# A decode attention kernel on one core: K of one pair loaded in two parts, the next V load held behind the first, waits of SyncE dropped, a clear cut into 32 pieces

## The chip, the cores and the metric

The kernel runs on one core of one Trainium2 chip, while nothing else runs beside it. The time is that of the device, in microseconds (us), the median of several runs. One further execution was taken by the hardware profiler; what is said of engines, waits and transfers comes from that one.

## The reference, cut to what matters

One decode step: 8 sequences, 32 heads, 4096 cached keys of 128 elements per head, all in bf16. An attention block and a small MLP work on the same normalized input, and both are added to x.

```python
xn = layernorm(x)                                   # x: [8, 1, 640]
q = (xn @ wq).reshape(8, 1, 32, 128).transpose(0, 2, 1, 3)
scores = einsum("bhqd,bhkd->bhqk", q, k_cache) * 128 ** -0.5
o = einsum("bhqk,bhkd->bhqd", softmax(scores), v_cache)
out = x + o.transpose(...).reshape(8, 1, 4096) @ wo \
        + gelu(layernorm(xn) @ w1 + b1) @ w2 + b2
```

`k_cache` and `v_cache` are [8, 32, 4096, 128] each. Every element of both is read once, 537 MB of the 552 MB that the kernel loads.

## The kernel before

**Pairs.** The work is cut into NQ = 32 pairs, i = 0 to 31, of one sequence and 8 heads. The K of a pair is one tile of 128 partitions x 256 columns x 128 elements (8.39 MB): 16 partitions per head, 256 keys (columns) in each partition, contiguous in memory. V has the same shape. "K of pair 4" in the change is the fourth one, i = 3.

**Buffers.** `S_sb` has three slots: K goes into `KA` for even i and `KB` for odd i, V always into `VS`. So K of pair i can be loaded when K of pair i - 2 has been used, and V of pair i when V of pair i - 1 has been used.

**Loads.** All large loads are issued by SyncE (`sp`) and run in one queue spread over 16 DMA engines. `load_k(i)` waits for `kt(i-2)` (the last transpose of that K by TensorE) and `km(i-2)` (the last reduction of that K by VectorE), then issues one DMA. `load_v(i)` waits for `pv(i-1)`, the last matmul of the pair before on V, and issues one DMA (two, of 192 and 64 columns, for i = 30). wq comes ahead of all of them; the MLP's weights and wo come last.

**Scores.** Columns 0 to 175 of a K tile are multiplied and reduced on VectorE, in three chunks (`dve_chunk`, the end of each is `km`). Columns 176 to 255 are transposed by TensorE (`pe_T`), copied by ScalarE (`act_T`) and multiplied by TensorE (`pe_QK`); VectorE folds the result (`dve_sel`), and this stands in VectorE's order before the third chunk. `k_ready(i)` is a tiny memset of `kr_sb` on GpSimd that waits for K; TensorE's transposes wait for it instead of the DMA. Then follow the maximum on VectorE, the exponentials on ScalarE, `pe_PV` on TensorE (256 matmuls per pair) and the normalization on GpSimd.

**Order.** The order is written out by hand: every step has a position and each engine takes its steps in the order of positions.

```python
for i in range(NQ):
    o = i * Q                       # Q = 100
    if i:
        at(o - 51, load_k, i)
    at(o + 50, load_v, i)
    at(o - 2, k_ready, i)
```

So SyncE's queue reads wq, K0, K1, V0, K2, V1, K3, V2, K4, V3 and so on; SyncE waits for one release after the other, in this order. VectorE, ScalarE and TensorE replay their steps from loops; SyncE and GpSimd run straight-line code.

**Start.** `consts_pool` runs on GpSimd at the start: index tiles (`iota`), then `zeros_sb` (128 x 128, bf16), `ones_sb`, `mx_sb`, `mb_sb` and `ones_f`. The ticket `consts` after the last is waited for by `pe_acc0`, the first matmuls into `ACC_ps`, and by `dve_max`. The memset of `ones_sb` also raises the semaphore `ld_vl` by one, a trick by which TensorE's loop can have a wait in every turn for the second part of V of i = 30.

All instructions are recorded by helper classes, so nearly all have line 111 in the profile; they are told apart by their tiles.

Of the kernel before, what the change touches and what calls it, by code (L numbers as in the profile page):

```python
# [14 lines left out]
P = 128  # L15
# [177 lines left out]
def bass_parallel_sum__gqa_block_cached__mixer_channel_mlp__decode_kernel(  # L193
# [21 lines left out]
    NQ = NHQ * B  # L215
# [5 lines left out]
    TPB = 8  # L221
    NS = 2
    LOOP0, LOOPN = 2, 15
    assert NKEY == 256 and NQ == 32
    SLOT = NKEY * DH
    KA, KB, VS = 0, 1, 2
# [6 lines left out]
    def jp_of(i):  # L233
        return 80

    def chunks(i):
        jd = NKEY - jp_of(i)
        n = 3
        return [(jd * c // n, jd * (c + 1) // n) for c in range(n)]

    def kslot(i):
        return KA if i % 2 == 0 else KB
# [8 lines left out]
    with ExitStack() as es:  # L251
        sb = lambda name, shape, dt: es.enter_context(nc.sbuf_tensor(name, shape, dt))
        ps = lambda name, shape, dt: es.enter_context(nc.psum_tensor(name, shape, dt))
        sem = lambda name: es.enter_context(nc.semaphore(name))

        S_sb = sb("S_sb", [P, 3, SLOT], BF)
        tile = [S_sb[:, s, :].rearrange("p (j d) -> p j d", d=DH) for s in range(3)]
# [6 lines left out]
        def scratch(n, rows=P, slot=KB):  # L264
            ap = part(slot, o_[slot], n, rows)
            o_[slot] += n + n % 2
            return ap
# [22 lines left out]
        zeros_sb = scratch(P)  # L290
        assert max(o_.values()) <= SLOT

        ones_sb = sb("ones_sb", [1, B], BF)
# [17 lines left out]
        mx_sb = sb("mx_sb", [P, 32], F32)  # L311
        mxT_sb = sb("mxT_sb", [P, 32], F32)
        mq_sb = sb("mq_sb", [P, 2], F32)
        mb_sb = sb("mb_sb", [P, 32], F32)
# [23 lines left out]
        pe, dve, act, sp, pool = (_Eng(sem(f"{n}_s")) for n in ("pe", "dve", "act", "sp", "pool"))  # L338
        pe2, act2 = _Eng(sem("pe2_s")), _Eng(sem("act2_s"))
        ld_s = [_Dma(sem(f"ld_s{s}")) for s in range(3)]  # L340
        ld_x, ld_b1, ld_b2, ld_wq, ld_w1, ld_w2a, ld_w2b, st_o = (
            _Dma(sem(n)) for n in ("ld_x", "ld_b1", "ld_b2", "ld_wq", "ld_w1", "ld_w2a", "ld_w2b", "st_o"))
        ld_vl = [_Dma(sem(f"ld_vl{q}")) for q in range(1, len(V_CUT) - 1)]
        ld_wl = [_Dma(sem(f"ld_wl{q}")) for q in range(2)]
        ld_wn = [_Dma(sem(f"ld_wn{q}")) for q in range(len(WN_CUT) - 1)]
        tk = {}
# [5 lines left out]
        def load(key, dma, dst, src, eng=None):  # L352
            tk[key] = dma.sig((eng or sp).dma_start(dst, src))

        def cache_src(cache, i):
            hq, b = divmod(i, B)
            return cache[b, hq * HS:(hq + 1) * HS].rearrange("h (p j) d -> (h p) j d", j=NKEY)

        def load_k(i):
            s = kslot(i)  # L360
            if i >= 2:
                sp.wait(tk[("kt", i - 2)], tk[("km", i - 2)])
            elif s == KB:
                sp.wait(tk["qmm"])
            tk[("k", i)] = ld_s[s].sig(sp.dma_start(tile[s], cache_src(A_k_cache, i)))

        def load_mlp():
            sp.wait(tk[("kt", NQ - 2)], tk[("km", NQ - 2)])
            load("w1", ld_w1, w1_sb, B_w1.rearrange("(p c) f -> p c f", c=DC))
            load("w2a", ld_w2a, w2_sb, B_w2[0:FB * P, :].rearrange("(p c) n -> p c n", c=FB))  # L370

        def load_v(i):
            sp.wait(tk["qmm"] if i == 0 else tk[("pv", i - 1)])
            if i != NQ - 2:
                tk[("v", i)] = [ld_s[VS].sig(sp.dma_start(tile[VS], cache_src(A_v_cache, i)))]
                return
            tk[("v", i)] = []
            for d, lo, hi in zip([ld_s[VS]] + ld_vl, V_CUT[:-1], V_CUT[1:]):
                if lo:
                    d.n += 1  # L380
                tk[("v", i)].append(
                    d.sig(sp.dma_start(tile[VS][:, lo:hi, :], cache_src(A_v_cache, i)[:, lo:hi, :])))
# [3 lines left out]
            load("b1", ld_b1, b1_sb, B_b1.rearrange("(o f) -> o f", o=1), act)  # L386

        def load_wl(q):
            sp.wait(tk[("kt", NQ - 1)], tk[("km", NQ - 1)])
            lo, hi = (0, HW) if q == 0 else (HW, HW + HS)  # L390
            tk[("wl", q)] = ld_wl[q].sig(sp.dma_start(
                woW_sb if q == 0 else woL_sb[:, 0, :],
                A_wo[lo * DH:hi * DH, :].rearrange("(p s) n -> p (s n)", p=P)))
# [15 lines left out]
        def consts_pool():  # L409
            pool.iota(iota_h, [[-HP, HS]], base=0, channel_multiplier=1)  # L410
            pool.iota(iota_w, [[-RW, HW]], base=0, channel_multiplier=1)
            tk["iota"] = pool.sig(pool.iota(iota_i, [[1, P]], base=0, channel_multiplier=-1))
            for d, (ap, v) in zip([None] + ld_vl + [None] * 2, (
                    (zeros_sb, 0.0), (ones_sb[:, :], 1.0), (mx_sb[:, :], 0.0), (mb_sb[:, :], 0.0))):
                inst = pool.memset(ap, v)
                if d is not None:
                    inst.call[3] = (d.sem, 1)
            tk["consts"] = pool.sig(pool.memset(ones_f[:, :], 1.0))
# [124 lines left out]
                qT_sb[:, hq * HS:(hq + 1) * HS, b][:, :, None].to_broadcast([P, HS, HP])))  # L543

        def k_ready(i):
            pool.wait(tk[("k", i)])
            tk[("kr", i)] = pool.sig(pool.memset(kr_sb[:, :], 0.0))

        def pe_qbc(i):
# [242 lines left out]
        at(-898, load, "b2", ld_b2, b2_sb, B_b2.rearrange("(o f) -> o f", o=1), act)  # L792
        at(-890, load, "wq", ld_wq, wq_sb, A_wq.rearrange("(p c) n -> p c n", c=DC))
        at(NQ * Q - 55, load_mlp)
        at(-897, load_w2b)
        at(-870, load_k, 0)
        at(-899, zero_w2b)
        at(-800, consts_pool)
        at(-795, idents)
        at(NQ * Q - 60, sel_pool)  # L800
# [15 lines left out]
        for i in range(NQ):  # L816
            o = i * Q
            last = i == NQ - 1
# [3 lines that stand above are left out]
            at(o - 52, qrep, i)  # L822
            at(o - 2, k_ready, i)
            at(o - 11, pe_qbc, i)
            at(o - 10.5, act_qbc, i)
            nt = jp_of(i) // TPB
            w = 42.0 / nt
            for t in range(nt):
                at(o + w * t, pe_T, i, t)
                at(o + w * (t + 0.4), act_T, i, t)  # L830
                at(o + w * (t + 1.5), pe_QK, i, t)
            at(o + 2, dve_chunk, i, 0)
            at(o + 26, dve_chunk, i, 1)
            at(o + 52, dve_sel, i, 0)
            at(o + 55, dve_sel, i, 1)
            at(o + 58, dve_chunk, i, 2)
            at(o + 84, dve_max, i)
            at(o + 90 if i else o + Q + 45, act_exp, i)
            at(o + Q + 48, pe_RS, i)
            at(o + Q + 57, dve_rinv, i)  # L840
            at(o + Q + 50, pe_PV, i)
            if not last:
                at(o + Q + 71, act_O, i)
            at(o + Q + 75, o_norm, i)
# [4 lines left out]
        for q in range(2):  # L849
            at(o + 50 + 0.1 * q, load_wl, q)  # L850
            at(o + 79.1 + 0.2 * q, fin_wl, q)
# [73 lines left out]
```

## Time and profile before

| | |
|---|---|
| median of 3 runs | 1282.03 us (1281.86 to 1282.14) |
| the profiled execution, from its first to its last instruction (its own time) | 1280.5 us |
| the median less that span | 1.5 us |
| busy: VectorE, TensorE matmul, ScalarE, GpSimd | 1103.8 (86%), 671.1 (52%), 476.6 (37%), 106.3 us (8%) |
| loaded from memory | 551.80 MB, 431 GB/s over the span |
| share of the 16 DMA engines taken by SyncE's queue | 99.7% |

In the lines of the profile, PE is TensorE's matmul, DVE VectorE, ACT ScalarE, POOL GpSimd, and SP SyncE; a q behind a name (SPq) is the engine's sequencer, which issues DMAs. A line of a timeline gives the start, the duration, the engine and operation, what is written from what, and in brackets the idle time ahead of it with what ended it. A line of the list of waits gives the total, the count and the longest. Times are in us from the span's start. DMA packets are counted where they start.

### The profile page before, as it was taken

Reading aid. Unit: us, or ns where it says so; the run is one execution under the profiler, and the core shown is the slowest. Engines: PE = TensorE matmul, PEld = TensorE weight load, DVE = VectorE, ACT = ScalarE, POOL = GpSimd, SP = SyncE. Lnnn points to the kernel's source line nnn. Section 1 sums busy time; section 2 is a strip of 40 time slices with the busy share of each in tenths; the row PEclk is TensorE's granted clock in tenths of the full one; section 3 lists DMA queues with packets and bytes.
Section 4 is the critical chain, followed back from the end, with each engine's and each line's share of the span. In section 5 each row is a group of like instructions: output and inputs, shape, how many; then the busy total and the mean of one; then the engine's idle time right before and its main releaser. Section 6 shows DMA issues by size and latency. Waiting matters only on the chain.

```text
span 1280.5 us, 34440 instructions
## 1 busy us (share of the span) xinstructions
PE 671.1 (52%) x13944; PEld 573.4 (45%) x13944; DVE 1103.8 (86%) x680; ACT 476.6 (37%) x904; POOL 106.3 (8%) x113
## 2 busy tenths in 40 slices
PE   1546555446545446545456554456454466464476
PEld 1435444335535345444345444345343355353365
DVE  1899999889888889888899888898888898888895
ACT  0524444233444233443234443234443234442331
POOL 0020010000000000000000000000000000000040
PEclk9755655566665565555565565566655555555655
DMA  9999999999999999999999999999999999999998
GB/s 419 431 426 435 426 436 432 442 426 436 432 440 428 434 432 438 432 432 430 436 438 426 434 434 442 426 434 434 438 430 430 430 440 436 428 432 436 433 437 361
DMA packets 10675, 551.99 MB, mean 431 GB/s; under 512 B 1244, under 2 KB 1445, under 8 KB 1702
## 3 DMA queue, kind: packets, MB, share of 16 engines
q1 hardware_dynamic: 10512, 551.70, 99.7%
q8 instruction: 9, 0.15, 0.0%
q10 hardware_dynamic: 150, 0.11, 0.0%
q14 instruction: 4, 0.03, 0.0%
HBM read 551.80 MB, written 0.01 MB: 431 GB/s over the span
## 4 chain that ended last, share of the span: by engine, by line
DMA 52%; DVE 36%; issue 11%; DVEq 0%; PE 0%; SPq 0%; ACT 0%
DMA S_sb<-in_A_k_cache_dram 51%; DVE S_sb L111 26%; DVE Sd_sb L111 8%; DMA S_sb<-in_A_wo_dram 2%; DVE S_ps L111 1%; DVE ri_sb L111 0%; DVEq L109 0%; PE ACC_ps L111 0%; DVE mx_sb L111 0%; SPq L111 0%; DVE mbT_sb L111 0%; DVE mxT_sb L111 0%; DVE mq_sb L111 0%; DVE mb_sb L111 0%; PE QB_ps L111 0%
## 5 line engine op out<-in xcount | busy, mean ns | idle before, releaser
L111 PE MATMUL TR_ps<-ident_bf,S_sb 128*128 128x128 bf16 (+1 forms) x2570 | 341.2, 273 | 354.1 <-POOL kr_sb L111 333.7
L111 DVE TENSOR_TENSOR S_sb<-S_sb,qbc_sb 128x7552 bf16<-128x7552 bf16 (+1 forms) x96 | 392.5, 4088 | 128.8 <-DMA S_sb<-in_A_k_cache_dram 128.4
L111 PEld LDWEIGHTS TR_ps<-ident_bf,S_sb 128*128 (+2 forms) x2570 | 243.6, 102 | 414.0 <-issue 338.2
L111 DVE TENSOR_REDUCE Sd_sb<-S_sb 128x59 f32<-128x3776 bf16 (+1 forms) x96 | 390.2, 4065 | 6.0
L111 ACT ACTIVATE KT_sb<-TR_ps 128x1024 bf16<-128x1024 bf16 x320 | 327.0, 1024 | 121.1 <-PE TR_ps L111 109.5
L111 PE MATMUL PV_ps<-P_sb,S_sb 128*128 128x8 bf16 x8192 | 224.0, 175 | 137.5 <-DMA S_sb<-in_A_v_cache_dram 134.5
L111 PEld LDWEIGHTS PV_ps<-P_sb,S_sb 128*128 128x128 bf16 x8192 | 221.4, 103 | 140.2 <-DMA S_sb<-in_A_v_cache_dram 137.0
L111 DVE TENSOR_TENSOR S_sb<-S_sb 128x3776 bf16<-128x3776 bf16 (+1 forms) x96 | 205.4, 2140 | 3.3
L111 ACT ACTIVATE P_sb<-Sd_sb,NB_sb 128x256 bf16<-128x256 f32 x256 | 126.3, 494 | 213.7 <-DVE NB_sb L111 213.7
L111 PE MATMUL S_ps<-qrep_sb,KT_sb 128*128 128x8 bf16 x2560 | 121.6, 177 | 51.6 <-ACT KT_sb L111 48.6
L111 ACT ACTIVATE oU_sb<-PV_ps 128x8 f32<-128x8 f32 x31 | 5.5, 178 | 376.8 <-PE PV_ps L111 376.8
L111 PEld LDWEIGHTS S_ps<-qrep_sb,KT_sb 128*128 128x128 bf16 x2560 | 91.3, 102 | 82.2 <-ACT KT_sb L111 41.6
L111 POOL TENSOR_TENSOR oT_sb<-oU_sb,ri_sb 128x8 bf16<-128x8 f32 x31 | 71.8, 2316 | 374.8 <-DVE S_sb L111 303.1
L111 POOL COPY qrep_sb<-qT_sb 128x128 bf16<-128x128 bf16 x32 | 19.2, 600 | 472.6 <-PE S_ps L111 454.0
L111 ACT ACTIVATION_READ_ACCUMULATOR P_sb<-Sd_sb,NB_sb 128x1 f32 x256 | 47.7, 186 | 0.0
L111 DVE TENSOR_TENSOR S_ps<-S_ps,mask_sb 128x320 f32<-128x320 f32 (+1 forms) x65 | 31.6, 486 | 2.6 <-PE S_ps L111 2.6
L111 DVE TENSOR_REDUCE Sd_sb<-S_ps 128x40 f32<-128x320 f32 x64 | 31.5, 492 | 2.2
L111 PE MATMUL QB_ps<-ident_bf,qrep_sb 128*128 128x128 bf16 x32 | 9.2, 286 | 40.7 <-DVE S_sb L111 21.2
L111 ACT ACTIVATE qbc_sb<-QB_ps 128x128 bf16<-128x128 f32 x32 | 8.9, 278 | 56.9 <-PE QB_ps L111 56.9
L111 POOL MEMSET kr_sb<- 128x1 f32 x32 | 3.2, 99 | 295.4 <-DMA S_sb<-in_A_k_cache_dram 295.4
L111 PEld LDWEIGHTS QB_ps<-ident_bf,qrep_sb 128*128 128x128 bf16 x32 | 3.3, 104 | 43.6 <-ACT oU_sb L111 29.3
L111 PE MATMUL CH_ps<-rs_sb,ones_f 128*128 128x8 f32 x64 | 16.7, 335 | 6.5 <-ACT P_sb L111 6.5
(73 smaller groups left out, 148.6 us busy)
## 6 DMA issues: line engine op xcount, KB each, us to landing
S_sb<-in_A_v_cache_dram SPq DMA_DIRECT2D x1, 6144.0 KB, 26.8
S_sb<-in_A_wq_dram SPq DMA_DIRECT2D x1, 5120.0 KB, 15.2
S_sb<-in_A_wo_dram SPq DMA_DIRECT2D x1, 2560.0 KB, 15.8
S_sb<-in_B_w_dram SPq DMA_DIRECT2D x1, 2160.0 KB, 30.3
S_sb<-in_B_w_dram SPq DMA_DIRECT2D x1, 2080.0 KB, 34.8
S_sb<-in_A_v_cache_dram SPq DMA_DIRECT2D x1, 2048.0 KB, 31.3
S_sb<-in_A_wo_dram SPq DMA_DIRECT2D x1, 1280.0 KB, 18.5
S_sb<-in_A_wo_dram SPq DMA_DIRECT2D x1, 800.0 KB, 20.0
```

Of the source, the lines that this page charges most:

```text
L111: inst = getattr(e, name)(*a, **k)
```

## The change

K of i = 3 (`ALIGN`) is loaded by two DMAs, of columns 0 to 231 (`ALIGN_CUT`) and 232 to 255; the second has a semaphore of its own, `ld_kz`. V of i = 2, the next load in SyncE's order, waits for the first part to have landed as well as for `pv(1)`. VectorE's chunks of that K wait for the first part, `k_ready(3)` for both. SyncE's waits for `kt`, in `load_k`, `load_mlp` and `load_wl`, are left out, those for `km` stay. `zeros_sb` is cleared by 32 memsets of 4 columns each instead of one of 128.

```diff
+    ALIGN, ALIGN_CUT = 3, 232
...
+        ld_kz = _Dma(sem("ld_kz"))
...
         def load_k(i):
             s = kslot(i)
             if i >= 2:
-                sp.wait(tk[("kt", i - 2)], tk[("km", i - 2)])
+                sp.wait(tk[("km", i - 2)])
             elif s == KB:
                 sp.wait(tk["qmm"])
-            tk[("k", i)] = ld_s[s].sig(sp.dma_start(tile[s], cache_src(A_k_cache, i)))
+            if i != ALIGN:
+                tk[("k", i)] = ld_s[s].sig(sp.dma_start(tile[s], cache_src(A_k_cache, i)))
+                return
+            n = ALIGN_CUT
+            assert n >= chunks(i)[-1][1]
+            tk[("k", i)] = ld_s[s].sig(sp.dma_start(tile[s][:, 0:n, :], cache_src(A_k_cache, i)[:, 0:n, :]))
+            tk["kz"] = ld_kz.sig(sp.dma_start(tile[s][:, n:, :], cache_src(A_k_cache, i)[:, n:, :]))

         def load_mlp():
-            sp.wait(tk[("kt", NQ - 2)], tk[("km", NQ - 2)])
+            sp.wait(tk[("km", NQ - 2)])
...
         def load_v(i):
             sp.wait(tk["qmm"] if i == 0 else tk[("pv", i - 1)])
+            if i == ALIGN - 1:
+                sp.wait(tk[("k", ALIGN)])
...
         def load_wl(q):
-            sp.wait(tk[("kt", NQ - 1)], tk[("km", NQ - 1)])
+            sp.wait(tk[("km", NQ - 1)])
...
-            for d, (ap, v) in zip([None] + ld_vl + [None] * 2, (
-                    (zeros_sb, 0.0), (ones_sb[:, :], 1.0), (mx_sb[:, :], 0.0), (mb_sb[:, :], 0.0))):
+            for c in range(0, P, 4):
+                pool.memset(zeros_sb[:, c:c + 4], 0.0)
+            for d, (ap, v) in zip(ld_vl + [None] * 2, (
+                    (ones_sb[:, :], 1.0), (mx_sb[:, :], 0.0), (mb_sb[:, :], 0.0))):
...
         def k_ready(i):
-            pool.wait(tk[("k", i)])
+            pool.wait(tk[("k", i)], tk["kz"] if i == ALIGN else None)
```

## The prediction

> **What bounds the kernel now.** I read the page first, then the list of waits, then the transfers, then the stretch in which the change works.
>
> ```profile
> span 1280.5 us, 34440 instructions
> ...
> DMA  9999999999999999999999999999999999999998
> ...
> DMA packets 10675, 551.99 MB, mean 431 GB/s; under 512 B 1244, under 2 KB 1445, under 8 KB 1702
> ...
> q1 hardware_dynamic: 10512, 551.70, 99.7%
> ...
> DMA 52%; DVE 36%; issue 11%; DVEq 0%; PE 0%; SPq 0%; ACT 0%
> ```
>
> The one queue that SyncE feeds keeps all 16 DMA engines busy for 99.7% of the span. The bytes are fixed, so only two things can move the time: the rate of the queue, or a hole in it. Engine waits say the same; the two that matter are waits for data:
>
> ```profile
> PE PV_ps L111 <- DMA S_sb<-in_A_v_cache_dram: 134.5, 28, 5.3
> ...
> DVE S_sb L111 <- DMA S_sb<-in_A_k_cache_dram: 128.4, 28, 15.1
> ```
>
> VectorE waits for K in 28 pairs and TensorE for V in 28 pairs: the compute engines trail the queue. The rate can be read off GpSimd, whose small memset starts when a K has landed (timeline of GpSimd):
>
> ```profile
> 133.19 0.10 POOL L111 MEMSET kr_sb<- 128x1 f32 x1 [1.97 <-DMA S_sb<-in_A_k_cache_dram]
> ...
> 171.90 0.10 POOL L111 MEMSET kr_sb<- 128x1 f32 x1 [6.34 <-DMA S_sb<-in_A_k_cache_dram]
> ...
> 210.60 0.10 POOL L111 MEMSET kr_sb<- 128x1 f32 x1 [10.32 <-DMA S_sb<-in_A_k_cache_dram]
> ```
>
> These are K of i = 3, 4 and 5. Between two of them lie two transfers of 8.39 MB: 210.60 - 171.90 = 38.70, so 19.35 us each. From 133 us to the end the queue runs at this pace, and a hole of x us put into it on the engine that is last makes the kernel x us longer. How much warning does a transfer have?
>
> ```profile
> S_sb<-in_A_k_cache_dram SPq DMA_DIRECT2D x32, 44.4
> S_sb<-in_A_v_cache_dram SPq DMA_DIRECT2D x31, 31.6
> ```
>
> From issue to landing less 19.35 us for the transfer itself, a K is usually issued 25 us and a V 12 us before its turn. That is the cover for everything small that happens at SyncE. But around i = 3 there is less (timeline of SyncE: K3, V2, K4, V3):
>
> ```profile
> 102.97 0.33 SPq L111 DMA_DIRECT2D S_sb<-in_A_k_cache_dram  x1
> 128.25 0.33 SPq L111 DMA_DIRECT2D S_sb<-in_A_v_cache_dram  x1
> 137.49 0.33 SPq L111 DMA_DIRECT2D S_sb<-in_A_k_cache_dram  x1
> 162.59 0.33 SPq L111 DMA_DIRECT2D S_sb<-in_A_v_cache_dram  x1
> ```
>
> V2 is issued at 128.25, and K3 lands at 133.19: the tightest place of the whole run, and exactly where the new wait is put.
>
> **The hold of V2: the term that counts.** Where does the last engine become free? Each engine ends its share of a transfer with a packet of 4 bytes. Two windows, 130.8 to 132.7 and 132.7 to 140 us, of the DMA view:
>
> ```profile
> DMA packets 32, 1.05 MB, mean 552 GB/s; under 512 B 16, under 2 KB 16, under 8 KB 16
> ```
> ```profile
> DMA packets 48, 3.15 MB, mean 431 GB/s; under 512 B 0, under 2 KB 0, under 8 KB 0
> ```
>
> All 16 end packets of K3 start before 132.7, none later. So the last engine is free for V2 at about 132.7, and the landing is visible to a waiter 0.5 us after that, at 133.19. V2 was issued 4.4 us ahead of that.
>
> After the change K3 comes as 232 and 24 of 256 columns. The 24 columns take 24/256 x 19.35 = 1.81 us, so the first part is visible at 133.19 - 1.81 = 131.38. SyncE's step from a seen release to the issue is short: VectorE's last work on pair 1 ends at 102.90, and K3 goes out at 102.97, so 0.07.
>
> ```profile
> 98.81 4.09 DVE L111 TENSOR_REDUCE Sd_sb<-S_sb 128x59 f32<-128x3776 bf16 x1
> ```
>
> V2 is then issued at about 131.45 instead of 128.25, 3.2 us later, and the last engine runs dry at 132.7, 1.25 us after the issue. Whether that makes a hole depends on the time from issue to data on an engine with nothing else queued. The only place that shows it is the start, where the wq load meets empty engines (timeline of SyncE, then half-microsecond windows; columns: window, length, clock, DMA share, GB/s by packets that start there):
>
> ```profile
> 0.74 0.38 SPq L111 DMA_DIRECT2D S_sb<-in_A_wq_dram  x1
> ```
> ```profile
> 1.00:1.50 0.50, 1.00 0.00 0
> 1.50:2.00 0.50, 1.00 3.19 919
> 2.00:2.50 0.50, 1.00 1.03 330
> 2.50:3.00 0.50, 1.00 0.28 82
> ...
> 4.00:4.50 0.50, 1.00 2.08 901
> 4.50:5.00 0.50, 1.00 0.19 82
> ```
>
> The first packets (40 KB) start 0.8 us after the issue at the earliest, the last of the 16 engines starts its own between 2.5 and 3.0 (82 GB/s over 0.5 us is one packet of 40 KB), and that engine's second packet starts between 4.5 and 5.0. At the queue's pace (8.39 MB in 19.35 us over 16 engines, 27.1 GB/s each) 40 KB takes 1.51 us, so its first packet counts as if it had begun at 3.0 to 3.5: 2.25 to 2.75 us after the issue, start-up included. Put to 131.45 that is 133.7 to 134.2, against 132.7 now: a hole of 1.0 to 1.5 us on the engine that then ends last. I take **1.25 us**.
>
> Its bounds: if data came 0.8 us after the issue on every engine, there would be no hole at all (0). If it came as late as V2's 4.4 us of warning just allows today, the hole would be 131.45 + 4.4 - 132.7 = **3.2 us**. I take the wq value, since that too is a full transfer handed to idle engines. The Trainium skill, "DMA: Bandwidth & Descriptors", section "Latency and other measured facts", gives about 0.6 us to the first byte for this kind of DMA; by that figure the 24 columns would cover the hold fully and this term would be zero, which the windows above, with the last engine starting 1.8 us or more after the issue, do not support.
>
> Who stands behind the new wait? On SyncE only K4 (137.49) and V3 (162.59); both keep their place, as 131.45 + 0.33 is over well before 137.49. V2 would land at 153.8 instead of 152.5, while TensorE starts on it only at 155.59 (the view was cut at 160 us, hence x166):
>
> ```profile
> 155.59 4.58 PE L111 MATMUL PV_ps<-P_sb,S_sb 128*128 128x8 bf16 x166
> ```
>
> So the release of V3 doesn't move, and V3 has spare time. From K4 on the queue simply runs 1.25 us late.
>
> **The split of K3.** One more issue (0.33 us) on an idle SyncE at 103.3: free. The two pieces together cost a little more than one. The kernel already does this with V of pair 30 (192 and 64 columns, two issues in 0.81 us):
>
> ```profile
> 1204.53 0.81 SPq L111 DMA_DIRECT2D S_sb<-in_A_v_cache_dram  x2
> ```
> ```profile
> S_sb<-in_A_v_cache_dram SPq DMA_DIRECT2D x1, 6144.0 KB, 26.8
> ...
> S_sb<-in_A_v_cache_dram SPq DMA_DIRECT2D x1, 2048.0 KB, 31.3
> ```
>
> The second part lands 31.3 - 26.8 + 0.4 = 4.9 us after the first; its bytes need 4.84. So **0.05 us** (bounds 0 to 0.1). VectorE may now start on K3 1.8 us earlier, but it is at K2 until 137.4, which is what lets K4 go at 137.49, so nothing is won. GpSimd's `k_ready(3)` waits for both parts and moves by no more than that 0.1 us, and so do TensorE's transposes behind it.
>
> **SyncE's dropped waits.** What they cost today:
>
> ```profile
> SPq L111 <- PE S_ps L111: 0.2, 1, 0.2
> ```
>
> 0.2 us, once in the run, and every K has 25 us of warning. Zero; without that cover it would be a few hundredths per K. The order stays, as the VectorE result waited for follows TensorE's scores of the same pair.
>
> **GpSimd's 32 pieces.** Small memsets start about 0.035 us apart and take 0.10 each:
>
> ```profile
> 0.24 0.10 POOL L910 MEMSET const-float32-0.0<- 128x1 f32 x1 [0.24 <-issue]
> 0.27 0.10 POOL L910 MEMSET const-float32-1.0<- 128x1 f32 x1
> ...
> 1.75 0.21 POOL L111 MEMSET S_sb<- 128x128 bf16 x1
> ...
> 7.99 0.22 PE L111 MATMUL ACC_ps<-S_sb 128*128 128x40 bf16 x1
> ```
>
> 32 of them last between 32 x 0.035 = 1.1 and 32 x 0.10 = 3.2 us in place of 0.21, so the constants are ready at 3.2 to 5.3 us. Their first reader is the matmul at 7.99, 2.7 us or more later. Zero.
>
> **Instruction fetches.** Fewer instructions on SyncE and 31 more on GpSimd move the moments at which their code is fetched over the same DMA engines. In the window 468 to 472 us:
>
> ```profile
> q14 instruction: 1, 0.01, 0.5%
> ```
>
> 0.5% of 16 engines over 4 us is 0.32 us of one engine. Today such a hit need not fall on the engine that is last; with all engines restarted together it may. Between -0.3 and +0.3; I take **0.1**.
>
> **Sum.** 1.25 + 0.05 + 0.1 = 1.4 us. On the profiled execution: 1280.5 + 1.4 = 1281.9 us of span. The runs' median is 1282.03, 1.5 us above that span (what lies around it), so 1283.4 us. That is 0.11% longer; 0.2%, about what a measurement of this kernel can tell from no change, is 2.56 us, so the bounds of that class are 1279.5 and 1284.6.
>
> **Rivals.**
>
> *No hole.* Engines that have been idle for a moment get V2 within about a microsecond, and the 24 columns cover it. For it: most packets at the start begin in 1.5:2.00, under 1.3 us after the issue. Against it: the end is set by the last engine, not by most. Time 1282.0 + 0.15 = 1282.2. Chance 0.20.
>
> *A long hole (ends slower).* Descriptors reach an engine still at work later than an idle one, and V2 takes its full 4.4 us. It decides if the issue-to-data time on the last engine is over 3.7 us (hole above 2.5). For it: nothing in the trace shows V2 ready sooner than 132.7 there. Against it: wq's 2.75. Time 1282.0 + 3.2 + 0.15 = 1285.4. Chance 0.13.
>
> *The rate changes with the engines in step.* Early in the run they were in step, having started together:
>
> ```profile
> 16.00:35.35 19.35, 1.00 1.00 431
> 35.35:54.70 19.35, 0.85 1.00 431
> ...
> 210.00:597.00 387.00, 0.57 1.00 433
> ```
>
> No gain there: 431 against 433 later, and one 64 KB packet more or less in 19.35 us is 3.4 GB/s, so equal. But rounding to 1 GB/s leaves room: 0.5 GB/s of 433 over the 1144 us that follow is 1.3 us, and a full 2 GB/s would be 5.3 us, either way. Faster: 1282.0 + 0 to 1.4 - 1.3 = 1280.8 to 1282.1 at half a GB/s, 1278.1 at the full 2. Chance 0.10, of which 0.07 is past 1279.5. The Trainium skill, same page, section "Where 436 GB/s comes from", puts the ceiling at 435 GB/s; the 433 measured leaves just that 2. Slower: all engines read the same offset of their rows at once and collide; 1283.4 + 5.3 = 1288.7 at the 431 of the early stretches. Chance 0.06. The same page's row "HBM row pitch at large powers of two" tells of such collisions between streams in lock step, with losses of half the rate; the early stretches show nothing of that size.
>
> **How the numbers follow.** Forecast 0.51 at 1283.4, no hole 0.20, long hole 0.13, faster rate 0.10, slower rate 0.06. Slower by over 0.2%: 0.13 + 0.06, and 0.01 of the forecast's upper edge, 0.20. Faster: 0.07. Same: 0.73. The range goes from 1280.8 (half a GB/s gained) to 1285.4 (the long hole) and leaves out the full rate changes.
>
> **What would show it.** SyncE's timeline: two K issues at 103, V2 at about 131.4. GpSimd's memset after K4 at 173.3 instead of 171.90 and after K5 at 212.0, the spacing still 38.70: the hole, and no change of rate. If K4 still comes at 172, there was no hole; at 175, the long one. A spacing under 38.60 would mean that being in step pays and break the forecast on the fast side. TensorE's first ACC_ps matmul stays near 8. A wait of VectorE or TensorE for something other than K or V near the top of the list would mean that the argument from the queue is wrong.

## The result and the profile after

| | before | after |
|---|---|---|
| median of 21 runs each | 1282.07 us (1281.86 to 1282.47) | 1283.61 us (1283.13 to 1285.19) |
| profiled execution | 1280.5 us | 1281.8 us |

The ratio is 1.0013, with a 95% interval from 1.0007 to 1.0019: the change makes the kernel about 1.5 us slower. The forecast was 1283.4 us. Two of the runs of after, 1284.91 and 1285.19, lie apart; the others end at 1284.07.

Not all of the 1.54 us between the medians lies inside the program. Every run has its own span on record. The run's time less its span is 1.69 us in after (median of 21 runs) and 1.33 in before (median of the 33 runs taken beside the first experiments), and the medians of the spans are 1281.9 and 1280.8. So 1.1 to 1.2 us are lost inside the span and nearly 0.4 outside it, where no view of the profile looks.

The page of after, to be held against the first fence of the prediction:

```profile
span 1281.8 us, 34442 instructions
...
q1 hardware_dynamic: 10656, 551.70, 99.6%
...
DMA 53%; DVE 36%; issue 11%; DVEq 0%; PE 0%; SPq 0%; ACT 0%
```

The queue is as full as before to a tenth of a per cent (one tenth is 1.3 us), and the chain still runs through the DMAs. In the list of waits the totals of the two waits for data have each grown by about a microsecond. SyncE's row for TensorE's `S_ps` is gone, and it has a new one, the hold itself: it waits for the first part of K3 until 131.4, where it stood waiting for `pv(1)` until 128.25 before.

```profile
PE PV_ps L111 <- DMA S_sb<-in_A_v_cache_dram: 135.6, 28, 5.2
DVE S_sb L111 <- DMA S_sb<-in_A_k_cache_dram: 129.6, 28, 15.1
```
```profile
SPq L109 <- DMA S_sb<-in_A_k_cache_dram: 27.5, 1, 27.5
```

SyncE's timeline (start, duration) shows two issues for K3, V2 at 131.43 instead of 128.25, and K4 and V3 within 0.2 us of their old places:

```profile
103.02 0.80 SPq L111 DMA_DIRECT2D S_sb<-in_A_k_cache_dram  x2
131.43 0.33 SPq L111 DMA_DIRECT2D S_sb<-in_A_v_cache_dram  x1
137.53 0.33 SPq L111 DMA_DIRECT2D S_sb<-in_A_k_cache_dram  x1
162.77 0.33 SPq L111 DMA_DIRECT2D S_sb<-in_A_v_cache_dram  x1
```

The DMA view from 98 to 140 us (size where it is not that of a whole tile, median us from issue to landing) gives the two parts of K3, and V2:

```profile
S_sb<-in_A_k_cache_dram SPq DMA_DIRECT2D x1, 7424.0 KB, 28.3
S_sb<-in_A_k_cache_dram SPq DMA_DIRECT2D x1, 768.0 KB, 29.8
S_sb<-in_A_v_cache_dram SPq DMA_DIRECT2D x1, 21.9
```

The second part lands 29.8 + 0.4 - 28.3 = 1.9 us after the first (its bytes need 1.81). V2 lands at 131.43 + 21.9 = 153.3; before it took 24.3 us and landed at 128.25 + 24.3 = 152.55. GpSimd's memset for i = 3, 4 and 5 of after, and for i = 31:

```profile
133.29 0.10 POOL L111 MEMSET kr_sb<- 128x1 f32 x1 [1.99 <-DMA S_sb<-in_A_k_cache_dram]
172.88 0.13 POOL L111 MEMSET kr_sb<- 128x1 f32 x1 [7.23 <-DMA S_sb<-in_A_k_cache_dram]
211.58 0.10 POOL L111 MEMSET kr_sb<- 128x1 f32 x1 [11.21 <-DMA S_sb<-in_A_k_cache_dram]
...
1218.04 0.10 POOL L111 MEMSET kr_sb<- 128x1 f32 x1 [9.87 <-DMA S_sb<-in_A_k_cache_dram]
```

From i = 3 to i = 4 it takes 39.59 us, 0.88 more than the 38.71 of before, and then 38.70 again. Before, the memset of i = 31 is at 1216.86. So the 1.3 us of the profiled execution divide as 0.10 ahead of i = 3, 0.88 from i = 3 to i = 4, 0.20 from there to i = 31 (1045.16 against 1044.96), and 0.12 behind it. Most of it is lost at one place, the one where the hold is. Windows of the DMA view there (window, length, clock, DMA share, GB/s by packets that start):

```profile
132.20:132.80 0.60, 0.50 3.72 1273
132.80:133.40 0.60, 0.50 1.46 546
133.40:134.00 0.60, 0.50 0.00 0
134.00:134.60 0.60, 0.50 0.00 0
134.60:135.20 0.60, 0.50 0.00 0
135.20:135.80 0.60, 0.50 3.02 1311
```

This is the restart: all engines take up V2 before 133.4, start nothing while their first 64 KB packets run, and come back close together after 135.2. Before, packets worth 546 and 328 GB/s started between 133.4 and 134.6.

### The profile page after: what moved, and what is told of

Its sections match the earlier page's. It is cut to its first block, busy times and chain, and to the rows that moved or that the text cites. A ratio compares the mean times of both kernels' runs of the same rounds, so it can differ in the third digit from the quotient of the medians.

```text
span 1281.8 us, 34442 instructions
## 1 busy us (share of the span) xinstructions
PE 670.3 (52%) x13944; PEld 572.3 (45%) x13944; DVE 1104.3 (86%) x680; ACT 476.1 (37%) x904; POOL 106.6 (8%) x144
## 4 chain that ended last, share of the span: by engine, by line
DMA 53%; DVE 36%; issue 11%; DVEq 0%; PE 0%; SPq 0%; ACT 0%
DMA S_sb<-in_A_k_cache_dram 51%; DVE S_sb L111 26%; DVE Sd_sb L111 8%; DMA S_sb<-in_A_wo_dram 2%; DVE S_ps L111 1%; DVE ri_sb L111 0%; DVEq L109 0%; PE ACC_ps L111 0%; DVE mx_sb L111 0%; SPq L111 0%; DVE mbT_sb L111 0%; DVE mxT_sb L111 0%; DVE mq_sb L111 0%; DVE mb_sb L111 0%; PE QB_ps L111 0%
## 6 DMA issues: line engine op xcount, KB each, us to landing
S_sb<-in_A_k_cache_dram SPq DMA_DIRECT2D x1, 7424.0 KB, 28.3
```

## The experiments

The theory: the hold leaves 1.81 us of bytes in the queue where an issue needs more than that to reach the last engine, and the hole that results is the whole cost. The rivals: the cost comes from another part (the split, the dropped waits, the 32 pieces, code fetches that moved), or from the engines' being in step. One measure is used for all: the time between GpSimd's memsets of i = 3 and i = 4, which is 38.71 in before. Each kernel was timed beside before (1282.00 to 1282.11 us in those runs). The V2 and memset columns come from one execution each; the column "outside the span" is the median, over the runs, of a run's time less its own span.

| kernel | V2 issued | V2, issue to landing | i = 3 to 4 | i = 3 to 31 | median us (runs) | outside the span | ratio to before [95%] |
|---|---|---|---|---|---|---|---|
| before | 128.25 | 24.3 | 38.71 | 1083.67 | 1282.07 (21) | 1.33 | |
| no hold | 128.44 | 24.4 | 38.64 | 1083.69 | 1282.11 (11) | 1.45 | 1.0000 [0.9991, 1.0009] |
| cut at 192 | 128.46 | 24.2 | 38.64 | 1083.62 | 1282.42 (11) | 1.65 | 1.0003 [0.9994, 1.0012] |
| cut at 200 | 129.07 | 24.0 | 39.12 | 1084.06 | 1282.76 (11) | 1.66 | 1.0005 [0.9997, 1.0014] |
| cut at 216 | 130.21 | 23.8 | 40.19 | 1085.23 | 1283.71 (11) | 1.70 | 1.0012 [1.0003, 1.0021] |
| split and hold alone | 131.36 | 22.5 | 40.00 | 1084.94 | 1283.24 (11) | 1.30 | 1.0009 [1.0000, 1.0018] |
| after, 43 pieces | 131.34 | 22.5 | 40.08 | 1085.15 | 1283.92 (11) | 1.71 | 1.0014 [1.0005, 1.0024] |
| after | 131.43 | 21.9 | 39.59 | 1084.75 | 1283.61 (21) | 1.69 | 1.0013 [1.0007, 1.0019] |
| hold, no split | 133.19 | 21.9 | 41.94 | 1087.03 | 1285.14 (11) | 1.48 | 1.0023 [1.0014, 1.0032] |
| hold, no split, 43 pieces | 133.23 | 21.9 | 41.34 | 1086.77 | 1285.11 (11) | 1.54 | 1.0023 [1.0014, 1.0032] |
| before, V2 behind VectorE | 137.54 | 21.8 | 45.47 | 1091.27 | 1289.74 (6) | 1.30 | 1.0062 [1.0049, 1.0074] |
| five holds | 131.58 | 21.8 | 39.75 | 1092.86 | 1289.76 (5) | 1.56 | 1.0056 [1.0043, 1.0070] |

**Without the hold.** After, less the new wait; split, dropped waits and 32 pieces stay.

```diff
         def load_v(i):
             sp.wait(tk["qmm"] if i == 0 else tk[("pv", i - 1)])
-            if i == ALIGN - 1:
-                sp.wait(tk[("k", ALIGN)])
```

> The changed kernel without the hold: V of i = 2 waits for pv(1) alone; K3 stays in two parts, the dropped waits and the 32 pieces stay. Hole theory (the time goes into the queue running dry between K3 and V2): no hole, so within 0.3 us of the kernel before, about 1282.2 us, and GpSimd's memset after K4 back at 171.9 to 172.0. Rival, the split and the two small edits cost it (moved code fetches, an extra piece): 1283.5 us, as the changed kernel.

```profile
133.59 0.10 POOL L111 MEMSET kr_sb<- 128x1 f32 x1 [2.26 <-DMA S_sb<-in_A_k_cache_dram]
172.23 0.10 POOL L111 MEMSET kr_sb<- 128x1 f32 x1 [6.57 <-DMA S_sb<-in_A_k_cache_dram]
```

38.64 between i = 3 and i = 4, and the same median as before. All that is not the hold costs nothing that the median can tell. In this one execution K3 is seen at 133.59, 0.4 us later than before, and the 0.4 is still there at i = 31.

**The hold without the split.** K3 in one DMA, V2 behind all of it: the cover of 1.81 us is gone.

```diff
-            if i != ALIGN:
+            if True:
                 tk[("k", i)] = ld_s[s].sig(sp.dma_start(tile[s], cache_src(A_k_cache, i)))
                 return
...
-            pool.wait(tk[("k", i)], tk["kz"] if i == ALIGN else None)
+            pool.wait(tk[("k", i)])
```

> The changed kernel with K3 in one DMA again and V of i = 2 held behind all of it. Hole theory: nothing is left in the queue to cover the time from the issue of V2 to its data, so the hole grows by just the 1.81 us of the 24 columns: 1283.6 + 1.8 = 1285.4 us (1285.0 to 1285.8), GpSimd's memset after K4 at 174.7. Rival, engines that start in step run at another rate or collide: they start in step just as much as in the changed kernel, so 1283.5 to 1284.0 us, with a spacing of K4 to K5 other than 38.70.

The DMA view and GpSimd's timeline:

```profile
S_sb<-in_A_v_cache_dram SPq DMA_DIRECT2D x1, 21.9
```
```profile
175.10 0.10 POOL L111 MEMSET kr_sb<- 128x1 f32 x1 [9.56 <-DMA S_sb<-in_A_k_cache_dram]
```

V2 lands at 133.19 + 21.9 = 155.1, so 2.55 us go by beyond the 19.35 of its bytes: this is what an issue to drained engines needs here, with the 0.5 us from the last data to the seen landing. K4 is then seen 20.0 us after V2, 0.65 too many. In that gap (window 164 to 172) one fetch of code runs:

```profile
q14 instruction: 1, 0.01, 0.2%
```

The Trainium skill, "DMA: Bandwidth & Descriptors", section "Queues, rings and completion order", says that an engine takes turns between the queues that have work for it, a packet at a time. By that rule a fetch delays the one engine that it falls on, which agrees with K4 coming late once; the rule gives no price. Read packet by packet, the trace gives one: the fetch takes 0.31 us of an engine, and the 64 KB packet behind it 2.66 us where 2.42 is usual, together 0.55 of the 0.65.

**The split and the hold alone.** Before, with nothing but these two; SyncE's waits and the single clear are kept.

```diff
+            if i == ALIGN - 1:
+                sp.wait(tk[("k", ALIGN)])
...
+            n = ALIGN_CUT
+            tk[("k", i)] = ld_s[s].sig(sp.dma_start(tile[s][:, 0:n, :], cache_src(A_k_cache, i)[:, 0:n, :]))
+            tk["kz"] = ld_kz.sig(sp.dma_start(tile[s][:, n:, :], cache_src(A_k_cache, i)[:, n:, :]))
...
-            pool.wait(tk[("k", i)])
+            pool.wait(tk[("k", i)], tk["kz"] if i == ALIGN else None)
```

> The kernel before with only the split of K3 and the hold of V2; SyncE keeps its waits for TensorE and the zeros are cleared by one memset. Hole theory: all of the loss is here, 1283.4 to 1283.7 us. Rival, the code fetches that the two small edits move now fall on the engine that ends last: 0.1 to 0.4 us less than the changed kernel, 1283.1 to 1283.4 us, or, as the code fetches near 469 and 982 us come back and may now hit the last engine, up to 0.3 us more.

```profile
173.26 0.10 POOL L111 MEMSET kr_sb<- 128x1 f32 x1 [7.41 <-DMA S_sb<-in_A_k_cache_dram]
```

1283.24 against 1282.11, and no run of the one reaches the runs of the other: the cost is there without the other parts. It came out below the 1283.4 to 1283.7 expected and inside the range of the rival. But the spans of this kernel and of after have the same median, 1281.9; the 0.37 us between them lie outside the span (1.30 against 1.69), so it is not the queue that makes them differ. Between i = 3 and i = 4 it loses 1.29 us, where the profiled execution of after lost 0.88 with the same edit in this place, and V2 takes 22.5 us to land instead of 21.9: the size of the hole differs from one execution to the next by some tenths, and one trace doesn't give it more finely.

**A larger second part.** With the cut at 192 columns, 64 columns (4.84 us of bytes) stay behind the hold.

```diff
-    ALIGN, ALIGN_CUT = 3, 232
+    ALIGN, ALIGN_CUT = 3, 192
```

> The changed kernel with the cut at column 192: 64 columns, 4.84 us, in the second part. Hole theory: from the issue of V2 to data on the last engine the changed kernel shows about 2.3 us, and 0.5 us go from the end of data to the seen landing; 4.84 us cover both, so no hole: 1282.1 to 1282.4 us, GpSimd's memset after K4 at 171.9 to 172.1. Rival, the hold or the split costs something by itself (a stall of SyncE, a second piece): 1283 us or more.

```profile
172.02 0.10 POOL L111 MEMSET kr_sb<- 128x1 f32 x1 [6.43 <-DMA S_sb<-in_A_k_cache_dram]
```

V2 goes out at 128.46, as it does without the hold: the first part lands at 102.96 + 25.4 = 128.4, and the hold hardly waits. The loss in the queue is gone. The median is 0.31 us above before, but the medians of the spans are 1280.7 and 1280.8: what is left lies outside the span.

**A middle cut.** 216 leaves 40 columns, 3.02 us of bytes, more than the 2.55 of a drained queue.

```diff
-    ALIGN, ALIGN_CUT = 3, 232
+    ALIGN, ALIGN_CUT = 3, 216
```

> The changed kernel with the cut at column 216: 40 columns, 3.02 us, in the second part. Hole theory: with 24 columns the hole was 0.8 us and with none 2.6 us, 1.8 apart as the 1.81 us of the columns, so the need is 2.6 us; 3.02 cover it: no hole, 1282.1 to 1282.6 us. Engines are nearly in step all the same, so the rival that being in step costs (or pays) by itself gives 1283.0 us or more (or less than 1281.8).

```profile
S_sb<-in_A_v_cache_dram SPq DMA_DIRECT2D x1, 23.8
```
```profile
173.49 0.10 POOL L111 MEMSET kr_sb<- 128x1 f32 x1 [7.78 <-DMA S_sb<-in_A_k_cache_dram]
```

The expectation that this is enough failed. V2 was issued 1.2 us earlier than in after and lands at 130.21 + 23.8 = 154.0, no earlier; i = 4 comes 1.48 us late, as with the smaller cover. So the 2.55 us hold for a queue that has run dry, and here 23.8 - 19.35 = 4.45 us went by. The prediction's "long hole" supposed that engines still at work get an issue later than idle ones. The trace shows something else (windows as above):

```profile
132.40:132.80 0.40, 0.50 2.83 1147
132.80:133.60 0.80, 0.50 0.00 0
133.60:134.00 0.40, 0.50 0.49 164
```

Read packet by packet, 15 of the 16 engines start on V2 between 131.23 and 132.74. Six of them, which worked on K3 until 132.2 or later, go over to V2 without a pause, 2.0 to 2.5 us after the issue, and their first packets take the usual 2.42 us. One engine starts only at 133.68, after all of K3 is done: the single packet of the last line, 64 KB that take 3.1 us. With seven more packets of 2.42 us it ends at 153.8 and sets the landing. So being at work on K3 does not by itself make an engine late, and one late engine of 16 is enough for the whole loss. Why that one, the trace doesn't show, as its packets don't name their engine.

**Between 216 and 192.** If 4.45 us is the need at such an issue, 56 columns (4.23 us) should come short by little.

```diff
-    ALIGN, ALIGN_CUT = 3, 232
+    ALIGN, ALIGN_CUT = 3, 200
```

> The changed kernel with the cut at column 200: 56 columns, 4.23 us, in the second part; V2 then goes out near 129.0. Theory now (V2 reaches an engine that has work queued up to 4 us after its issue, a drained one after 2.1 to 2.7): 129.0 + 4.0 is 133.0, 0.3 after the last engine runs out at 132.7: a hole of 0 to 0.4 us, 1282.2 to 1282.8 us; V2 from issue to landing 23.6 to 24.3 us. Old theory (2.3 us from issue to data, so 2.6 us of cover are enough): 1282.1 us, no hole. Rival, each hold costs about 1 to 1.5 us whatever the cover, since it restarts the engines: 1283.3 to 1283.8 us.

```profile
S_sb<-in_A_v_cache_dram SPq DMA_DIRECT2D x1, 24.0
```
```profile
172.48 0.10 POOL L111 MEMSET kr_sb<- 128x1 f32 x1 [6.76 <-DMA S_sb<-in_A_k_cache_dram]
```

24.0 - 19.35 = 4.65 us, and 0.41 us lost between i = 3 and i = 4. (Where nothing is lost, in before, at 192 and without the hold, the same difference is 4.85 to 5.05 and is only the time until K3 is done and seen.) Cut by cut the loss falls from 1.48 to 0.41 to nothing as the cover grows from 3.02 to 4.23 to 4.84 us.

**A queue that has run fully dry.** Before with one edit, which keeps V2 until VectorE is done with K2 (137.4 us).

```diff
         def load_v(i):
             sp.wait(tk["qmm"] if i == 0 else tk[("pv", i - 1)])
+            if i == 2:
+                sp.wait(tk[("km", 2)])
...
-            at(o + 50, load_v, i)
+            at(o + (59 if i == 2 else 50), load_v, i)
```

> The kernel before with one edit: V of i = 2 is held until VectorE's km(2), near 137.5 us, when all engines have been without work for 4 us. Theory now: a drained queue gives data on the last engine 2.1 us after the issue, so the queue stands still from 132.7 to 139.6: 6.9 us, 1288.7 to 1289.3 us, and V2 lands 21.7 to 22.1 us after its issue. Rival, a hole is partly won back later since the compute engines have time to spare: less, 1287 us or under. Rival, V2 needs 3 to 4 us on drained engines too: 1290 us and more.

```profile
S_sb<-in_A_v_cache_dram SPq DMA_DIRECT2D x1, 21.8
```
```profile
137.60:138.20 0.60, 0.50 0.00 0
138.20:138.80 0.60, 0.50 3.28 1092
138.80:139.40 0.60, 0.50 1.20 437
139.40:140.00 0.60, 0.50 0.51 218
```

Issued at 137.54 to engines that had nothing else, V2 needs 21.8 - 19.35 = 2.45 us, as in after and without the split. The windows show how: a 64 KB packet in 0.6 us is 109 GB/s, so ten engines start 0.7 to 1.3 us after the issue, four by 1.9, and the last two 1.9 to 2.5 us after it. The Trainium skill, "DMA: Bandwidth & Descriptors", section "Latency and other measured facts", gives about 0.6 us to the first byte for this kind of DMA. Here the first engines start somewhat later than that, and the last ones, which set the landing, take three to four times as long. The loss from i = 3 to i = 4 is 45.47 - 38.71 = 6.76 us; the median is 7.7 us up, 0.4 above the range expected, because a further 0.84 us goes between i = 4 and i = 31 (1045.80 against 1044.96):

```profile
217.41 0.10 POOL L111 MEMSET kr_sb<- 128x1 f32 x1 [9.86 <-DMA S_sb<-in_A_k_cache_dram]
256.12 0.10 POOL L111 MEMSET kr_sb<- 128x1 f32 x1 [9.89 <-DMA S_sb<-in_A_k_cache_dram]
295.18 0.10 POOL L111 MEMSET kr_sb<- 128x1 f32 x1 [10.23 <-DMA S_sb<-in_A_k_cache_dram]
333.99 0.10 POOL L111 MEMSET kr_sb<- 128x1 f32 x1 [9.98 <-DMA S_sb<-in_A_k_cache_dram]
```

38.71, then 39.06 and 38.81: single steps are late, while the usual step stays 38.70. Nothing in the kernel distinguishes these pairs. After has 0.20 us of this kind; no hold and the cuts at 192, 200 and 216 have 0.1 or less. In the late steps the packets themselves are slower, those of most engines at once. A window of 16 packets inside the step of 39.06, in before and in this run:

```profile
284.20:286.60 2.40, 0.50 1.01 437
```
```profile
284.20:286.60 2.40, 0.50 1.09 437
```

1.09 of 16 engines over 2.40 us is 2.62 us for each 64 KB packet, against 2.42. Counted packet by packet between 145 and 1250 us, 72 packets of this run take more than 2.48 us, 40 of after, but 2 of before and at most 5 without the hold, at the three other cuts, and with the split and the hold alone. So engines that have been restarted together do slow each other now and then; by what, no run isolates.

**Moving the code fetch.** GpSimd's fetch near 167 us lies just behind the hold. With 43 pieces of 3 columns instead of 32 of 4, eleven more instructions move it to 97 us.

```diff
-            for c in range(0, P, 4):
-                pool.memset(zeros_sb[:, c:c + 4], 0.0)
+            for c in range(0, P, 3):
+                pool.memset(zeros_sb[:, c:min(c + 3, P)], 0.0)
```

> The changed kernel with the zeros cleared in 43 pieces (3 columns each) instead of 32. Theory: GpSimd's code is fetched in blocks of 8 KB, and the fetch near 167 us, after the hold, hits one of the engines that the hold has put in step and makes it the last by up to 0.66 us; with 11 more instructions the same fetch comes before the hold, near 55 to 75 us, and the hold takes it up: 1283.0 to 1283.4 us, 0.1 to 0.6 below the changed kernel. Rival, the fetch costs nothing: 1283.6 us.

1283.92 beside the 1283.61 of after, well inside both intervals and not the 0.1 to 0.6 less that was expected; i = 4 came 1.37 us late in this execution (133.21, then 173.29), so a tenth or two from the fetch could not be seen. The same edit on the kernel without the split, where K4 had come 0.65 late:

```diff
-            if i != ALIGN:
+            if True:
...
-            for c in range(0, P, 4):
-                pool.memset(zeros_sb[:, c:c + 4], 0.0)
+            for c in range(0, P, 3):
+                pool.memset(zeros_sb[:, c:min(c + 3, P)], 0.0)
...
-            pool.wait(tk[("k", i)], tk["kz"] if i == ALIGN else None)
+            pool.wait(tk[("k", i)])
```

> K3 in one DMA, V of i = 2 held behind all of it, zeros in 43 pieces. With 32 pieces this kernel took 1285.14 us, and K4 landed 0.66 us later after V2 than the pace of the queue gives, with the code fetch at 167 us between them. Theory that this fetch costs it: 1284.4 to 1284.7 us, GpSimd's memset after K4 near 174.5 instead of 175.10. Rival, that the delay of K4 has another cause: 1285.1 us, 175.1.

```profile
174.54 0.10 POOL L111 MEMSET kr_sb<- 128x1 f32 x1 [8.93 <-DMA S_sb<-in_A_k_cache_dram]
213.25 0.10 POOL L111 MEMSET kr_sb<- 128x1 f32 x1 [9.88 <-DMA S_sb<-in_A_k_cache_dram]
252.19 0.10 POOL L111 MEMSET kr_sb<- 128x1 f32 x1 [10.12 <-DMA S_sb<-in_A_k_cache_dram]
291.08 0.10 POOL L111 MEMSET kr_sb<- 128x1 f32 x1 [10.06 <-DMA S_sb<-in_A_k_cache_dram]
```

V2 lands at 133.23 + 21.9 = 155.1 as it did there, and K4 comes at 174.54 instead of 175.10: the 0.65 is gone with the fetch. But of the three steps that follow the last two take 38.94 and 38.89, so 0.43 us is lost later, and the median is the same, 1285.11 against 1285.14. In these two executions the fetch delays K4; removing it did not shorten the run.

**Five holds.** If each hold makes a hole and being in step gains nothing, five should cost about five times as much; if a hold also gains a little, the gains add up.

```diff
-    ALIGN, ALIGN_CUT = 3, 232
+    ALIGN, ALIGN_CUT = (3, 9, 15, 21, 27), 232
...
-            if i != ALIGN:
+            if i not in ALIGN:
...
-            if i == ALIGN - 1:
-                sp.wait(tk[("k", ALIGN)])
+            if i + 1 in ALIGN:
+                sp.wait(tk[("k", i + 1)])
...
```

> The changed kernel with five such holds: K of i = 3, 9, 15, 21 and 27 in two parts, V of the pair before each held behind the first. Hole theory: every hold costs its own hole; the queue restarted after 0.8 us in the changed kernel and after 1.3 us in the one with the hold alone, so four more holds add 3.3 to 5.2 us: 1286.9 to 1288.8 us. Rival, the loss is paid once, for bringing the engines into step: they are in step already, 1283.6 to 1284.2 us. GpSimd's memsets should come 38.70 us apart over two pairs, except across each hold, where it is 0.8 to 1.3 more.

```profile
366.93 0.10 POOL L111 MEMSET kr_sb<- 128x1 f32 x1 [9.99 <-DMA S_sb<-in_A_k_cache_dram]
407.09 0.10 POOL L111 MEMSET kr_sb<- 128x1 f32 x1 [11.85 <-DMA S_sb<-in_A_k_cache_dram]
...
834.02 0.10 POOL L111 MEMSET kr_sb<- 128x1 f32 x1 [10.00 <-DMA S_sb<-in_A_k_cache_dram]
875.35 0.10 POOL L111 MEMSET kr_sb<- 128x1 f32 x1 [11.81 <-DMA S_sb<-in_A_k_cache_dram]
```

Behind i = 9 the step is 40.16, behind i = 21 41.33. Over 38.70 the five steps lose 1.05, 1.46, 0.72, 2.63 and 1.99 us, 7.85 in all, 1.6 each; 1.3 us more are spread over other steps. The profiled execution was the slowest of the five runs (1291.52 us); the median is 7.7 us above before, five times the 1.5 of after and 1 us more than the range expected. At the later places SyncE has two loads behind the hold: V8 goes at 365.02 and K10 at 365.39, both set free by the same wait. That may be why those holes are larger on average, but nothing here isolates it.

No version ran faster than before.

## Why the prediction was right, step by step

- **The hold is the term that counts: shown.** Removing it alone gives the time of before (1282.11 us); adding it and the split alone to before gives 1283.24.
- **V2 at about 131.45: 131.43. K4 and V3 keep their places: 137.53 and 162.77.** V2 landing at 153.8: 153.3.
- **A hole of 1.25 us (bounds 0 to 3.2): within bounds, too large for the profiled execution and about right over all.** V2's landing is 0.8 us later than before. In the four kernels with the same hold at this place, i = 4 lost 0.88, 1.05, 1.29 and 1.37 us in one trace each.
- **Issue to data 2.25 to 2.75 us, from the wq load: of the right size.** The prediction counts up to the data; issue to landing holds another 0.5 us, which has to come off. Then after, the run without the split, the drained one and the five holds show 1.95 to 2.05 us, and the two others with the same hold 22.5 - 19.35 - 0.5 = 2.65. What was wrong is the idea that one figure holds for any issue. At 216 the prediction's own rule would have left a hole of 0.3 us at most (130.21 + 2.75 - 132.7), and 1.48 were lost, because one engine came late.
- **"A long hole": its price was not paid, and its mechanism is not what the trace shows.** At the cut of 216 all engines were still at work when V2 was issued; six took it up without a pause, 15 had it by 132.74, when the last of K3 was done, and one late engine set the time. In after the loss stays at about 1 us instead of 3.2.
- **"No hole": fell** with the 0.88 us and with the run without the hold.
- **"The rate changes": fell as a steady change.** From 210 to 597 us after moves 434 GB/s where before moved 433, and the step stays 38.70. Sharper: from i = 5 to i = 31 after takes 1006.46 us and before 1006.26. That the engines slow each other when in step is seen only in the short stretches above, 0.2 us in after.

```profile
210.00:597.00 387.00, 0.57 1.00 434
```

- **The split, SyncE's waits and the pieces at nothing: right together,** by the run without the hold. The split's 0.05 us (at most 0.1) is not confirmed: K3 is seen at 133.16 to 133.25 in the four traces where it comes in one piece, and at 133.21 to 133.59 in the eight where it comes in two. The 32 memsets take 1.06 us, as the lower bound had it, and the matmul that reads them first came at 8.47 instead of 7.99 without consequence, since the queue sets the pace:

```profile
1.74 1.06 POOL L111 MEMSET S_sb<- 128x4 bf16 x32
```
```profile
8.47 0.21 PE L111 MATMUL ACC_ps<-S_sb 128*128 128x40 bf16 x1
```

- **Code fetches 0.1 us (between -0.3 and +0.3): the idea holds, the bound was too narrow.** The prediction said that a fetch need not matter as long as the engines are apart, and may when they have been restarted together. K4 follows V2 by 0.2, 0.45 and 0.65 us more than 19.35 in the three traces with a restart and the fetch between the two (after, five holds, no split), and by 0.1 or less in those with only one of them (split and hold alone and the two with 43 pieces; no hold and the cuts at 192 and 200).
- **Not in the sum: steps that come late further on,** 0.20 us in after and up to 0.84 with a queue that had run dry.
- **Not in the sum: the time outside the span.** The prediction took the 1.5 us around the span as fixed, from one execution's span and the median of other runs. Run by run it is 1.3 before and 1.7 after. It stays at 1.30 with the split and the hold alone, so the dropped waits and the pieces have a part in it; no run takes them singly.
- **The total was closer than its terms, and part of that is luck.** The forecast had 1.4 us, all of it inside the span. The runs lost 1.1 to 1.2 there and nearly 0.4 outside. (By its own terms the lower edge of the range is 1282.0 - 1.3 = 1280.7, not 1280.8.)

Open: why the hole varies between executions and between holds (0.7 to 2.6 us), why one engine starts late at the cut of 216, and what makes the packets slower for a moment once the engines have been restarted together. The first two would need to know which of the 16 engines each packet ran on.

## What to carry to other kernels

Where one queue holds the DMA engines at over 99%, a wait put ahead of an issue is paid for as soon as the work left in the queue is shorter than the time from issue to data on the last engine; here 4.23 us of queued bytes still lost 0.41 us and 4.84 lost nothing. The start of the kernel, or an issue to idle engines, shows less (about 2.5 us here), so it is no safe measure of that lead. Count the remaining edits (a split, dropped waits, small instructions on an engine with slack) at nothing if the trace shows slack, confirm it with one run that takes out only the edit with a cost, and compare the runs' own spans as well as their times.

## What the runs showed that was not expected

- An issue made 1.2 us earlier did not land earlier: 130.21 + 23.8 = 154.0 against 131.43 + 21.9 = 153.3, and 153.9 in the run with the split and the hold alone. One engine of 16 started late.
- One load reaches its 16 engines over a wide stretch even when all are idle: the first after 0.7 to 1.3 us, the last after 1.9 to 2.5.
- Engines restarted together run no faster (38.70 us a step, as before), and for short stretches slower; the queue that had stood longest lost a further 0.84 us in single late steps.
